# Attention and a mixture of experts in one kernel: three spaced turns of GpSimd in an attention step, and another order of the products in it

## Chip, core and metric

One core of one Trainium2 chip. The metric is the device time of an execution in microseconds, the median of several runs.

## What is computed

Sliding-window attention of 8 sequences of 576 tokens with 8 heads of 64, four heads with a plain window of 32 and four with a window that is dilated by 4, and behind it a mixture of 8 experts of which every token takes two:

```python
rel = pos[:, None] - pos[None, :]
mask_plain = (rel >= 0) & (rel < 32)
mask_dil = (rel >= 0) & (rel < 32 * 4) & (rel % 4 == 0)
scores = where(mask, q @ k.T / sqrt(64), -1e9)
attn = exp(scores - scores.max(-1)); attn /= attn.sum(-1) + 1e-9
x = (attn @ v).transpose(0, 2, 1, 3).reshape(4608, 512)

noisy = x @ w_gate + log1p(exp(x @ w_noise)) * noise
top2 = the two largest of 8;  top2_w = softmax over the two
for e in range(8):
    for k in range(2):
        rows = top2[:, k] == e
        out[rows] += top2_w[rows, k] * (relu(x[rows] @ w1[e]) @ w2[e])
```

w1 is 512 x 1024 and w2 1024 x 512 for each expert; all is fp32.

## The kernel before

**Stages.** The attention runs in 24 steps (`NS = 6 * U`). Three steps make a group of one kind of head (even groups dilated, odd plain), two groups a unit of two sequences, U = 4 units. The results x go to a scratch in DRAM (`xs`), the gate is computed in between, and each token's entry (where x lies, its weight, its row) is scattered into a table (`tab`) sorted by expert. Then the experts run one after the other (`up` and `down`): rows of x are gathered through the table, split into a high and a low part, multiplied in three fp32r products, and the results are scattered with an add into the output.

**A step.** Step i works on several tiles of 384 rows: `qk(i)` adds the mask (a product with the identity) and the scores into one PSUM tile `s` and has VectorE take the row maxima and subtract them into the SBUF tile `a` (one buffer); `expo(i)` takes the exponential on ScalarE; `ptr(i-1)` transposes the probabilities in six 128x128 blocks, ScalarE copies them out; `pv(i-1)` multiplies with v in blocks of 32 query rows, VectorE divides by the sums into `x` (three buffers); `move_x` and `store_x` bring x to its layout and to DRAM; `x_transpose(i-2)` transposes x, `gate_mm(i-2)` multiplies it with the gate's weights in blocks of 32 columns; `gate_front` transposes the logits back in three steps of every unit, when both kinds of head are there. Mask, transposes and gate_front use 128 columns of the PE array per product, scores, pv and gate_mm 32.

**Order.** The program is written in the order in which each engine executes it; there is no scheduler. The loop over i emits the parts of a step in a fixed order. Each step has two slots (2i and 2i+1, `fillers`), at which transfers and one-off work that were planned with `at(slot, ...)` are emitted; `SP` issues the loads of q, k and v, the stores of x, the clearing of the output and the weights.

**Gate.** `gate(t0, n)` is a generator for n tiles of 128 tokens. `micro(n)` advances the live generators by a few operations wherever it is called in a step (n, or 2n at `rate` 2); a `yield 1` holds one until the next slot. At its end come the scatters, one for each tile: `fill_slots(0, t)` in the generator, `fill_slots(1, t)` put into `backlog`.

**Turns of GpSimd.** A scatter or a gather of x for the first expert (`first_blocks`) needs a turn. `new_slot(scatters, speed)` is called at the end of every slot and grants turns; those left over from the slot before go to the backlog. `pool_turn` first emits a spacer: for the first turn of a grant a 1x1 copy of the latest `x` (so that GpSimd waits until it is there, `late["x"]`), otherwise a small memset (`pace`). Four turns are granted in every second slot:

```python
new_slot((4, 0)[kb % 2], 1 if kb < 28 else 2)
```

**Experts.** PE's order is `up` and `down` of blocks of rows; other work is planned with `plan(t, f)` by a clock that advances with the columns PE was given (2400 a us). For the first expert the table is read in three pieces (`idx_late`, up to rows 384, 896 and the rest), the gathers take turns, `split_first` transposes the rows on PE. What is left of the backlog is emitted by `some_of_slots` and `rest_of_slots`; from `start + 42` on the second expert's entries are read, for which all scatters must be done.

Of the kernel before, what the change touches and what calls it, by code (L numbers as in the profile page):

```python
# [25 lines left out]
U = 4  # L26
# [20 lines left out]
def attention_moe_kernel(ctx, tc, qt, kp, kd, vpl, vdl, w_gate, w_noise, noise, w1, w2, out, CAPS=(1216, 1216, 1216, 1184, 1184, 1152, 1152, 1152), SPLITS=(0, 384, 896)):  # L47
# [27 lines left out]

    late = {}
    late["stage"] = ctx.enter_context(tc.tile_pool(name="stage", bufs=2, side="right"))
# [213 lines left out]

    fresh, backlog = [True], []

    def new_slot(scatters, speed=1):
        if scatters:
            while room[0] > 0 and backlog and not experts[0]:
                pool_turn()
                backlog.pop(0)()
            room[0], fresh[0] = scatters, True
        rate[0] = speed  # L300
        held.clear()

    def pace(yes=True):

        if yes and late["x"] is not None:
            gpsimd.tensor_copy(spacer, late["x"])  # L306
        else:
            gpsimd.memset(spacer, 0.0)
# [44 lines left out]

    def qk(k):
        g, st = divmod(k, 3)
        ty = 1 - g % 2
        s = aps.tile([128, 8, 2, 64], F32, name="s", tag="s")
        for e in (0, 4):
            n = min(4, 6 - e)
            tensor.matmul(s[:, e:e + n], lhsT=identb,  # L360
                          rhs=masks[ty][:, 6 * st + e:6 * st + e + n].unsqueeze(2).to_broadcast([128, n, 2, 64]),
                          start=True, stop=False, skip_group_check=True)
        for e in range(6):
            for qd in range(4):
                if ty == 0:
                    x = qd // 2
                    b, ub = divmod(12 * st + 6 * (qd % 2) + e, 18)
                else:
                    x = qd
                    b, ub = divmod(6 * st + e, 9)  # L370
                tensor.matmul(s[32 * qd:32 * qd + 32, e], lhsT=QV[ty][:, b, x, 32 * ub:32 * ub + 32],  # L371
                              rhs=KV[ty][:, :, b, x, 32 * ub:32 * ub + 64],
                              start=False, stop=True, skip_group_check=True)
        a = sm.tile([128, 2, 6, 64], F32, name="a", bufs=1)
        mx = sm.tile([128, 6, 2], F32, name="mx")
        vector.tensor_reduce(mx, s[:, 0:6], axis=AX.X, op=OP.max)
        vector.tensor_tensor(a.rearrange("p y e c -> p e y c"), s[:, 0:6], mx.unsqueeze(3).to_broadcast([128, 6, 2, 64]), op=OP.subtract)
        SB[k] = a

    def expo(k):  # L380
# [19 lines left out]
    def pv(k):  # L400
# [3 lines left out]
        o = aps.tile([128, 2, 512], F32, name="o", tag="o")  # L404
        for hh in range(4):
            for r, a, jp, b, ub in blocks(st, ty):
                qd, c0 = (r, hh) if r < 4 else (2 * (r - 4) + hh // 2, 4 + hh % 2)
                if ty == 0:
                    y, src = hh // 2, 2 * (hh % 2) + a
                    rhs = VP[b][:, :, ub // 2, hh]  # L410
                else:
                    y, src = a, hh
                    rhs = VD[:, :, 3 * st + jp, hh, y]
                tensor.matmul(o[32 * qd:32 * qd + 32, c0 // 3, 130 * (c0 % 3):130 * (c0 % 3) + 130],
                              lhsT=pt[:, y, 128 * jp + 32 * src:128 * jp + 32 * src + 32],
                              rhs=rhs, start=True, stop=True, skip_group_check=True)
# [343 lines left out]
    X = {}  # L760
    GT = {}

    def gather(e, t):
        r0, rn = TLS[e][t] if e != "o" else (0, 128)
        g = gp_.tile([128, 4, 128], F32, name="g")
        if e == 0:

            rows = 2304 * (next((i for i in range(U - 1) if r0 + rn <= SPLITS[i]), U - 1) + 1)
            for c in range(2):
                gpsimd.indirect_dma_start(  # L770
                    out=g[0:rn, 2 * c:2 * c + 2].rearrange("p c d -> p (c d)"), out_offset=None, in_=xs[0:rows],
                    in_offset=bass.IndirectOffsetOnAxis(ap=IX[0][0][0:rn, t, c:c + 1], axis=0))
            GT[e, t] = g
            return
# [141 lines left out]
    for g in range(2 * U):  # L916
# [7 lines left out]
    fronts = {6 * u + 6 + st: (u, st) for u in range(U) for st in range(3)}  # L924
    def idx_late(before, a, b, then):
# [26 lines left out]
    def split_first(bi, t):  # L952
        xsplit(0, bi, t)()
        done[bi] += 1

# [11 lines left out]
    at(29, lambda: (new_idx(0), gens.append(idx_late(list(gens), 0, SPLITS[1], lambda: x_block(0)))))  # L967
    at(41, lambda: gens.append(idx_late(list(gens), SPLITS[1], SPLITS[2], lambda: x_block(1))))
    at(2, setup_a)
# [30 lines left out]
    def fillers(kb):  # L1000
        slot[0] = kb + 1
        for f in fill.pop(kb, []):
            f()
        new_slot((4, 0)[kb % 2], 1 if kb < 28 else 2)

    NS = 6 * U
    early[0] = False
    for i in range(NS + 2):
        slot[0] = 2 * i
        early[0] = True  # L1010
        micro(2)
# [19 lines left out]
        if 1 <= i <= NS:  # L1031
            pv(i - 1)
        micro(2)
# [8 lines left out]
    for f in fronts.values():  # L1042
        gate_front(*f)
# [34 lines left out]
    for e in range(E):  # L1078
# [19 lines left out]
        if first:  # L1098
# [22 lines left out]

            plan(start + 2.5, some_of_slots)
            plan(start + 20, lambda: gens.append(rest_of_slots()))
# [110 lines left out]
```

## Time and profile before

| | |
|---|---|
| runs | 1027.26 us median of 3 (1026.15 to 1028.05) |
| span of the profiled execution | 1086.8 us |
| attention, up to the first product of the experts | 227.24 us of the span |
| experts | 859.56 us of the span |
| busy in the span | PE 1011.7, DVE 465.7, ACT 319.4, POOL 534.5 us |
| DMA | 132.95 MB, 122 GB/s in the mean |

The profiled execution's own time is known by its span alone, from the first to the last instruction: 59.5 us more than the median of the other runs. Durations below are from it; the clock is the granted clock of TensorE, 1.00 or a half at any moment, averaged over a stretch. Busy times of an engine are without its waits. A releaser "issue" means that nothing in the profile shows what the instruction waited for, "remote" that a semaphore was awaited that no instruction of the profile is seen to raise. A `DMA_INDIRECT` of POOL is a gather or scatter, its bar the time in which the descriptors are made and not that of the transfer.

### The profile page before, as it was taken

What the parts mean: (1) busy time and instruction counts of PE and PEld (TensorE: products, weight loads), DVE (VectorE), ACT (ScalarE), POOL (GpSimd) and SP (SyncE); (2) the same over time, 40 slices, a digit from 0 to 9 for tenths busy, and PEclk for the clock granted to TensorE, in tenths of its full rate; (3) what the DMA queues carried; (4) which work ended last, traced back from release to release, by engine and by line L of the source; (5) the groups of instructions that cost most, each with busy time, mean ns of one, the idle gap of its engine ahead of it and who ended that gap; (6) DMA issues with size and microseconds to landing.
All of it is one profiled execution on the core that took longest, in us unless ns stands there. A gap on an engine that the chain in (4) does not pass through costs nothing. (4 is left out here: it accounts for less than half of the span.)

```text
span 1086.8 us, 18768 instructions
## 1 busy us (share of the span) xinstructions
PE 1011.7 (93%) x7274; PEld 855.7 (79%) x7275; DVE 465.7 (43%) x1060; ACT 319.4 (29%) x609; POOL 534.5 (49%) x727
## 2 busy tenths in 40 slices
PE   6896877778989999999999999999999999999996
PEld 4774655567878989988997889788978888888885
DVE  7673635635225444344434352435353434343221
ACT  6673534622113322222223131312131222222110
POOL 7004243455776655755644564466455645553112
PEclk9998887878999999999999999999999999999999
DMA  8898687455255243533533352426242623453123
GB/s 280 313 315 278 194 283 257 151 164 186 43 96 129 54 109 85 109 84 86 91 85 85 86 131 50 102 64 135 38 112 52 137 39 108 75 119 72 24 28 45
DMA packets 79214, 132.95 MB, mean 122 GB/s; under 512 B 31648, under 2 KB 41296, under 8 KB 77840
## 3 DMA queue, kind: packets, MB, share of 16 engines
q1 hardware_dynamic: 56768, 92.56, 27.6%
q0 software_dynamic: 22352, 39.15, 19.6%
q8 instruction: 58, 0.95, 0.4%
q14 instruction: 36, 0.29, 0.1%
HBM read 92.11 MB, written 39.54 MB: 121 GB/s over the span
## 5 line engine op out<-in xcount | busy, mean ns | idle before, releaser
L826 PE MATMUL up<-x,w1h 128*128 128x512 f32 (+4 forms) x1536 | 396.7, 344 | 10.9 <-issue 8.2
L778 POOL DMA_INDIRECT g<-xs,ixi x258 | 269.7, 1045 | 84.0 <-issue 78.6
L826 PEld LDWEIGHTS up<-x,w1h 128*128 128x128 f32 x1536 | 273.1, 189 | 37.2 <-issue 8.7
L826 PE MATMUL up<-x,w1l 128*128 128x384 f32 (+4 forms) x768 | 263.4, 343 | 0.0
L868 PE MATMUL dn<-w2h,hh 128*128 128x512 f32 x576 | 225.5, 392 | 0.0
L868 PE MATMUL dn<-w2l,hh 128*128 128x512 f32 x576 | 224.7, 390 | 0.0
L868 PE MATMUL dn<-w2h,hl 128*128 128x512 f32 x576 | 224.6, 390 | 0.0
L832 DVE SCALAR_TENSOR_TENSOR hl<-up,hh 128x384 fp32r<-128x384 f32 (+2 forms) x192 | 106.7, 557 | 249.1 <-ACT hh L830 187.0
L830 ACT ACTIVATE hh<-up 128x384 fp32r<-128x384 f32 (+4 forms) x192 | 94.6, 498 | 298.7 <-PE up L826 248.7
L845 POOL DMA_INDIRECT out_rows<-y,ixs x67 | 107.3, 1602 | 141.4 <-DVE y L877 119.0
L826 PEld LDWEIGHTS up<-x,w1l 128*128 128x128 f32 x768 | 145.4, 189 | 11.8
L877 DVE TENSOR_SCALAR y<-dn,ixs 128x512 f32<-128x512 f32 x63 | 47.3, 751 | 188.2 <-PE dn L868 163.5
L868 PEld LDWEIGHTS dn<-w2h,hl 128*128 128x128 f32 x576 | 108.4, 188 | 22.7
L868 PEld LDWEIGHTS dn<-w2h,hh 128*128 128x128 f32 x576 | 108.5, 188 | 22.0
L868 PEld LDWEIGHTS dn<-w2l,hh 128*128 128x128 f32 x576 | 108.5, 188 | 21.8
L797 ACT CAST x<-xr 128x512 fp32r<-128x512 f32 x67 | 40.5, 605 | 216.0 <-DVE xr L795 175.8
L306 POOL COPY spacer<-hh 1x1 f32<-1x1 f32 x72 | 26.4, 366 | 131.9 <-ACT hh L830 131.6
L628 POOL DMA_INDIRECT tab<-en,si x72 | 71.8, 998 | 36.1 <-issue 16.2
L798 DVE TENSOR_TENSOR x<-xr,x 128x512 fp32r<-128x512 f32 x67 | 44.7, 667 | 17.9 <-ACT x L797 12.4
L371 PE MATMUL s<-kt,qt 128*32 128x128 f32 x1152 | 41.2, 288 | 9.9 <-DMA qt<-in_qt 5.4
L371 PEld LDWEIGHTS s<-kt,qt 128*32 128x32 f32 x1152 | 32.5, 115 | 20.3 <-issue 19.6
L708 DVE TENSOR_TENSOR w1l<-ws,w1h 128x1024 fp32r<-128x1024 f32 x32 | 38.8, 1218 | 20.8 <-ACT w1h L706 10.9
(186 smaller groups left out, 867.2 us busy)
## 6 DMA issues: line engine op xcount, KB each, us to landing
ws<-in_moe_w SPq DMA_DIRECT2D x36, 512.0 KB
ws<-in_moe_w SPq DMA_DIRECT2D x112, 128.0 KB
out_rows<-zero SPq DMA_DIRECT2D x38, 256.0 KB
vd<-in_vdl SPq DMA_DIRECT2D x24, 390.0 KB
vp<-in_vpl SPq DMA_DIRECT2D x16, 585.0 KB
qt<-in_qt SPq DMA_DIRECT2D x14, 576.0 KB
xs<-x SPq DMA_DIRECT2D x24, 256.0 KB
kt<-in_kd SPq DMA_DIRECT2D x16, 320.0 KB
```

Of the source, the lines that this page charges most:

```text
L371: tensor.matmul(s[32 * qd:32 * qd + 32, e], lhsT=QV[ty][:, b, x, 32 * ub:32 * ub + 32], rhs=KV[ty][:, :, b, x, 32 * ub:32 * ub + 64], star ...
L628: ins = gpsimd.indirect_dma_start(out=tab, out_offset=bass.IndirectOffsetOnAxis(ap=si[:, kq, t:t + 1], axis=0), in_=en[:, kq, t], in_offse ...
L708: return lambda: vector.tensor_tensor(b, s, a.bitcast(F32), op=OP.subtract)
L778: gpsimd.indirect_dma_start(out=g[:, j], out_offset=None, in_=xq, in_offset=bass.IndirectOffsetOnAxis(ap=IX[e][1][:, r0 // 32 + j:r0 // 32 ...
L797: scalar.copy(xh[:, :, o:o + rn], xr[:, :, 0:rn])
L798: return lambda: vector.tensor_tensor(xl[:, :, o:o + rn], xr[:, :, 0:rn], xh[:, :, o:o + rn].bitcast(F32), op=OP.subtract)
L826: tensor.matmul(p[:, 0:n], lhsT=a[:, 128 * f:128 * f + 128], rhs=b[:, kc, 0:n], start=(i == 0), stop=(i == 11))
L830: scalar.activation(hh[:, f, 0:n], p[:, 0:n], AF.Relu)
L832: vector.scalar_tensor_tensor(hl[:, f, 0:m], p[:, 0:m], 0.0, hh[:, f, 0:m].bitcast(F32), op0=OP.max, op1=OP.subtract)
L845: ins = gpsimd.indirect_dma_start(out=out, out_offset=bass.IndirectOffsetOnAxis(ap=sc[0:rn, t, 1:2], axis=0), in_=y[0:rn], in_offset=None, ...
L868: tensor.matmul(p[0:rn], lhsT=a[:, f, o:o + rn], rhs=b[:, f % 2], start=(i == 0), stop=(i == 23))
L877: vector.tensor_scalar(y[0:rn], p[0:rn], wsc, None, op0=OP.mult)
```

## The change

It has five parts.

1. Turns: two in even slots and one in odd ones (four in each from slot 47 on). The first spacer of an odd slot copies from `a`, the difference of scores and maxima of this step, and so waits for VectorE's subtraction. A gather for the first expert is split: each half of the columns takes a turn of its own.
2. Order within a step: x_transpose (of step i-3 now, i-2 before), mask, ptr, gate_front, then scores, gate_mm (i-3), pv, with the exponential emitted behind pv. move_x is behind ptr. Fronts of the first three units come one step later.
3. pv goes over the first four blocks of rows for all four heads, and then over the last two.
4. The maxima are taken in two parts, after four and after six score blocks.
5. Gates: seven of 6 and 3 tiles in the attention (five before), double speed of `micro` from slot 16 on (28 before). Six of the slots left over are planned at 10.5 us of the experts' clock (2.5 before).

```diff
-    def new_slot(scatters, speed=1):
+    def new_slot(scatters, speed=1, at=None):
...
-            room[0], fresh[0] = scatters, True
+            room[0], fresh[0], mark[0] = scatters, True, late["x"] if at is None else at
...
-    def pace(yes=True):
+    def pace(yes=True, at=None):
+        at = late["x"] if at is None else at
-        if yes and late["x"] is not None:
-            gpsimd.tensor_copy(spacer, late["x"])
+        if yes and at is not None:
+            gpsimd.tensor_copy(spacer, at)
...
-        pace(fresh[0] and not experts[0])
+        pace(fresh[0] and not experts[0], mark[0])
...
+    def mask_scores(k):     # the two products with the identity, out of qk
...
+            if e in (3, 5):
+                e0 = e - e % 4 if e == 5 else 0
+                vector.tensor_reduce(mx[:, e0:e + 1], s[:, e0:e + 1], axis=AX.X, op=OP.max)
-        vector.tensor_reduce(mx, s[:, 0:6], axis=AX.X, op=OP.max)
...
+        late["a"] = a[0:1, 0, 0, 0:1]
...
-        for hh in range(4):
-            for r, a, jp, b, ub in blocks(st, ty):
+        bl = list(blocks(st, ty))
+        for hh, rows in [(hh, bl[0:4]) for hh in range(4)] + [(hh, bl[4:6]) for hh in (0, 2, 1, 3)]:
+            for r, a, jp, b, ub in rows:
...
-            yield from wait_turn()
-            room[0] -= 1
-            gather(0, t)
+            for c in range(2):
+                yield from wait_turn()
+                gather(0, t, c)
...
-    for t0, n, kb in ((0, 9, 17), (9, 9, 29), (18, 6, 39), (24, 3, 41), (27, 6, 51)):
+    for t0, n, kb in ((0, 6, 16), (6, 3, 18), (9, 6, 28), (15, 3, 30), (18, 6, 40), (24, 3, 42), (27, 6, 50)):
...
-        new_slot((4, 0)[kb % 2], 1 if kb < 28 else 2)
+        new_slot((2, 1)[kb % 2] if kb < NK - 1 else 4, 1 if kb < 16 else 2, late["a"] if kb % 2 else None)
...
-        if i < NS:
-            qk(i)
-        micro(2)
-        if i >= 2:
-            move_x(i - 2)
+        if 3 <= i < NS:
+            x_transpose(i - 3)
+        micro(2)
+        if i < NS:
+            mask_scores(i)
         micro(2)
         if 1 <= i <= NS:
             ptr(i - 1)
         micro(2)
+        for f in fronts.pop(i, []):
+            gate_front(*f)
+        if i >= 2:
+            move_x(i - 2)
         micro(2)
         fillers(2 * i)
         if i >= 2:
             store_x(i - 2)
-            x_transpose(i - 2)
         if i < NS:
-            expo(i)
+            qk(i)
         micro(2)
+        if 3 <= i < NS:
+            gate_mm(i - 3)
         if 1 <= i <= NS:
             pv(i - 1)
-        micro(2)
-        if i >= 2:
-            if i in fronts:
-                gate_front(*fronts.pop(i))
-            gate_mm(i - 2)
+        if i < NS:
+            expo(i)
+        for k in {NS: (NS - 3, NS - 2), NS + 1: (NS - 1,)}.get(i, ()):
+            micro(2)
+            x_transpose(k)
+            gate_mm(k)
...
-            plan(start + 2.5, some_of_slots)
+            plan(start + 10.5, some_of_slots)
...
-                    some()
-                    tick(1200)
+                    some()
+                    for t in range(*BLS[0][bi][0:2]):
+                        split_first(bi, t)
```

(`split_first` does its work only if both halves have been issued and it was not done before.)

More of the change, by code (lines that the diff above doesn't have):

```diff
@@ L74, in attention_moe_kernel @@
     ixp = ctx.enter_context(tc.tile_pool(name="ixp", bufs=3))
-    late = {}
+    late = {"x": None, "a": None}
     late["stage"] = ctx.enter_context(tc.tile_pool(name="stage", bufs=2, side="right"))
@@ L290, in attention_moe_kernel @@
     room, held, rate = [0], set(), [1]
-    fresh, backlog = [True], []
-    def new_slot(scatters, speed=1):
+    fresh, backlog, mark = [True], [], [None]
+    def new_slot(scatters, speed=1, at=None):
         if scatters:
@@ L352, in attention_moe_kernel @@
     SB, PE_, PT, XG, XT, GS = {}, {}, {}, {}, {}, {}
-    def qk(k):
+    SC = {}
+    def mask_scores(k):
         g, st = divmod(k, 3)
         ty = 1 - g % 2
-        s = aps.tile([128, 8, 2, 64], F32, name="s", tag="s")
+        s = SC[k] = aps.tile([128, 8, 2, 64], F32, name="s", tag="s")
         for e in (0, 4):
@@ L362, in qk @@
                           start=True, stop=False, skip_group_check=True)
+    def qk(k):
+        g, st = divmod(k, 3)
+        ty = 1 - g % 2
+        s = SC.pop(k)
+        mx = sm.tile([128, 6, 2], F32, name="mx")
         for e in range(6):
@@ L760, in attention_moe_kernel, with gather @@
     X = {}
-    GT = {}
-    def gather(e, t):
+    GT, GOT = {}, {}
+    def gather(e, t, c=None):
         r0, rn = TLS[e][t] if e != "o" else (0, 128)
-        g = gp_.tile([128, 4, 128], F32, name="g")
[L766 to L774, printed above, removed]
+        if e == 0:
+            GOT[t] = c == 1
+            if c == 0:
+                GT[e, t] = gp_.tile([128, 4, 128], F32, name="g")
+            rows = 2304 * (next((i for i in range(U - 1) if r0 + rn <= SPLITS[i]), U - 1) + 1)
+            gpsimd.indirect_dma_start(
+                out=GT[e, t][0:rn, 2 * c:2 * c + 2].rearrange("p c d -> p (c d)"), out_offset=None, in_=xs[0:rows],
+                in_offset=bass.IndirectOffsetOnAxis(ap=IX[0][0][0:rn, t, c:c + 1], axis=0))
+            return
+        g = gp_.tile([128, 4, 128], F32, name="g")
         if e != "o":
@@ L923, in attention_moe_kernel @@
                 at(s0 + 7 + 2 * (i // 3), f)
-    fronts = {6 * u + 6 + st: (u, st) for u in range(U) for st in range(3)}
+    fronts = {6 * u + 7 + st: [(u, st)] for u in range(U - 1) for st in range(3)}
+    fronts[6 * U + 1] = [(U - 1, 0), (U - 1, 1)]
+    fronts[6 * U + 2] = [(U - 1, 2)]
     def idx_late(before, a, b, then):
@@ L952, in split_first @@
     def split_first(bi, t):
-        xsplit(0, bi, t)()
-        done[bi] += 1
+        if GOT.get(t) and (0, t) in GT:
+            xsplit(0, bi, t)()
+            done[bi] += 1
     def x_block(bi):
@@ L962, in x_block @@
             plan(US_X[bi - 1] + 3.0 * i, lambda t=t: split_first(bi, t))
-    for t0, n, kb in ((0, 9, 17), (9, 9, 29), (18, 6, 39), (24, 3, 41), (27, 6, 51)):
+    for t0, n, kb in ((0, 6, 16), (6, 3, 18), (9, 6, 28), (15, 3, 30), (18, 6, 40), (24, 3, 42), (27, 6, 50)):
         at(kb, lambda t0=t0, n=n: gens.append(gate(t0, n)))
     L0 = 12 * (U - 1)
-    at(29, lambda: (new_idx(0), gens.append(idx_late(list(gens), 0, SPLITS[1], lambda: x_block(0)))))
-    at(41, lambda: gens.append(idx_late(list(gens), SPLITS[1], SPLITS[2], lambda: x_block(1))))
+    at(30, lambda: (new_idx(0), gens.append(idx_late(list(gens), 0, SPLITS[1], lambda: x_block(0)))))
+    at(42, lambda: gens.append(idx_late(list(gens), SPLITS[1], SPLITS[2], lambda: x_block(1))))
     at(2, setup_a)
@@ L1025, in attention_moe_kernel @@
             store_x(i - 2)
-            x_transpose(i - 2)
+        if i < NS:
[3 more added lines that the diff above has]
+            gate_mm(i - 3)
+        if 1 <= i <= NS:
+            pv(i - 1)
         if i < NS:
             expo(i)
-        micro(2)
-        if 1 <= i <= NS:
-            pv(i - 1)
-        micro(2)
-        if i >= 2:
-            if i in fronts:
-                gate_front(*fronts.pop(i))
-            gate_mm(i - 2)
+        for k in {NS: (NS - 3, NS - 2), NS + 1: (NS - 1,)}.get(i, ()):
+            micro(2)
+            x_transpose(k)
+            gate_mm(k)
         micro(2)
@@ L1041, in attention_moe_kernel @@
     early[0] = True
-    for f in fronts.values():
+    for f in sum(fronts.values(), []):
         gate_front(*f)
```

1 line of the change is left out of this document (removed).

## Prediction

> **What bounds the kernel now.** I read the page's head first, then the stage table (busy time by stretch, cut where attention steps begin), then PE's order inside one step, then the timeline of a slow step, and last the costs by line. The page: PE is the engine to follow, and its granted clock dips only in the first quarter.
>
> ```profile
> span 1086.8 us, 18768 instructions
> ...
> PE 1011.7 (93%) x7274; PEld 855.7 (79%) x7275; DVE 465.7 (43%) x1060; ACT 319.4 (29%) x609; POOL 534.5 (49%) x727
> ...
> PEclk9998887878999999999999999999999999999999
> ```
>
> Stage table: length, then busy time of PE, PEld, DVE, ACT, POOL, clock, DMA share, GB/s.
>
> ```profile
> 41.90:47.28 5.38, 5.38 (x129) 4.61 (x126) 3.40 (x8) 4.48 (x12) 0.00 (x0) 1.00 0.94 350
> 59.30:65.31 6.01, 6.01 (x137) 4.82 (x130) 3.67 (x9) 3.99 (x9) 0.00 (x0) 1.00 0.95 316
> 83.44:100.97 17.53, 11.12 (x132) 7.91 (x130) 5.21 (x17) 4.15 (x9) 8.95 (x17) 0.74 0.93 310
> 100.97:110.93 9.96, 7.70 (x134) 5.20 (x130) 2.98 (x8) 3.96 (x9) 4.12 (x7) 0.94 0.71 224
> 116.93:128.56 11.63, 7.37 (x133) 5.97 (x127) 5.24 (x20) 4.80 (x14) 4.25 (x8) 0.75 0.73 229
> 128.56:135.34 6.78, 6.16 (x139) 5.00 (x138) 5.93 (x39) 4.69 (x13) 2.22 (x4) 0.93 0.42 73
> 140.71:155.37 14.66, 9.75 (x132) 5.91 (x130) 4.18 (x13) 3.95 (x9) 8.55 (x16) 0.82 0.97 322
> 155.37:167.83 12.46, 10.06 (x133) 7.66 (x130) 4.09 (x9) 3.97 (x9) 4.26 (x8) 0.67 0.81 261
> 173.84:190.87 17.03, 9.59 (x139) 6.63 (x135) 7.38 (x46) 5.05 (x16) 8.17 (x12) 0.70 0.61 211
> 197.62:227.24 29.62, 19.76 (x250) 14.47 (x249) 14.28 (x45) 14.61 (x35) 14.42 (x25) 0.79 0.45 137
> 59.30:197.62 138.32, 108.30 (x1949) 82.23 (x1943) 73.23 (x289) 67.39 (x170) 40.69 (x73) 0.85 0.78 258
> 227.24:1086.80 859.56, 836.24 (x4153) 722.30 (x4151) 336.89 (x614) 198.33 (x336) 458.94 (x583) 0.99 0.40 88
> ```
>
> A step without work on GpSimd is all PE: 5.38 us, or 6.01 with a gate_front. The steps in which GpSimd issues four or eight scatters last 10 to 17.5 us. The experts, from 227.24 on, are PE at full clock, and the change leaves that arithmetic alone. Inside a slow step:
>
> ```profile
> 147.36 0.38 PE L414 MATMUL o<-vp,pt 128*32 128x130 f32 x2 [0.99 <-issue]
> 148.09 0.27 PE L414 MATMUL o<-vp,pt 128*32 128x130 f32 x1 [0.36 <-issue]
> ```
> ```profile
> 148.04 0.98 POOL L628 DMA_INDIRECT tab<-en,si  x1 [0.16 <-issue]
> 149.02 0.09 POOL L308 MEMSET spacer<- 1x1 f32 x1
> 149.32 0.96 POOL L628 DMA_INDIRECT tab<-en,si  x1 [0.21 <-issue]
> ```
>
> While scatters follow each other every 1.27 us, PE gets an instruction every 0.7 us and waits for nothing that the profile names. The step with two scatters (128.56) loses little.
>
> **How this stands to the runs.** The span is 59.5 us longer than the median of 1027.26, so something in this execution is not in the timed ones. The six steps above with four or more indirect transfers last 83.3 us; three clean steps of 5.38 and three or four of 6.01 in their places (12, 13, 18, 19 have a front, 15 and 21 have none) make 34.8: 48.5 us too much. The closing stretch has 29.62 us with 19.76 of PE at clock 0.79, some 14 too much, and one gap in the experts is 7.69:
>
> ```profile
> 247.75 1.01 PE L826 MATMUL up<-x,w1h 128*128 128x384 f32 x2 [7.69 <-issue]
> ```
>
> Together about 70 us of stalls of one kind, against 59.5 of excess. The experts' matmuls run back to back, so they can't give it. I conclude that nearly all of these stalls belong to the profiled execution and that some 11 us of them are left in a timed run. The forecast is for the timed run; the span itself I expect to fall more, by 30 to 50 us.
>
> **The change, part by part.**
>
> *128-column products first.* Now a step is mask (128), scores (32), transposes of p and x (128), pv (32), front (128), gate_mm (32):
>
> ```profile
> 59.30 0.50 PE L360 MATMUL s<-mask,identb 128*128 128x512 bf16 x2
> 59.73 1.52 PE L371 MATMUL s<-kt,qt 128*32 128x128 f32 x48
> 61.18 0.87 PE L396 MATMUL pp<-ident,pe 128*128 128x128 f32 x6
> 61.89 0.82 PE L449 MATMUL xtp<-ident,x 128*128 128x128 f32 x6
> 62.64 1.79 PE L414 MATMUL o<-vd,pt 128*32 128x130 f32 x48
> 64.36 0.55 PE L509 MATMUL gt<-ident,gs 128*128 128x128 f32 x3
> ```
>
> The front makes a step 0.63 longer, but three transposes are half of the six that take 0.71 (61.18 to 61.89), 0.36. The other 0.27 is two more changes between 128 and 32 columns: about 0.13 each. A step has four changes, six with a front; afterwards two. That saves 0.27 or 0.54: over steps 3 to 23 (eleven or twelve without, nine with) 8 us, if PE stays the limit.
>
> *The chain that this closes.* The transposes of p come before the next scores now, so scores, maximum, subtraction, exponential, transposes, scores is a loop within one step, where before it had a step of slack.
>
> ```profile
> L377 DVE TENSOR_TENSOR a<-s,mx 128x768 f32<-128x768 f32 x24 | 23.0, 958 | 2.4
> L376 DVE TENSOR_REDUCE mx<-s 128x12 f32<-128x768 f32 x24 | 22.9, 956 | 45.0 <-remote 20.6 <-PE s L371 12.2 <-PE xtp L449 6.2
> L382 ACT ACTIVATE pe<-a 128x768 f32<-128x768 f32 x24 | 22.6, 940 | 4.7 <-DVE a L377 4.2
> L510 DVE TENSOR_REDUCE lg<-gt 128x48 f32<-128x192 f32 x12 | 4.2, 350 | 2.7 <-PE gt L509 2.7
> ```
>
> From 192 elements (350 ns) to 768 (956) a reduction costs 1.05 ns an element and 148 ns fixed. The second part (256) is then 0.42. The loop: 0.42 + 0.96 + 0.94 + 0.71 + 1.45 (scores, 59.73 to 61.18) = 4.48, with four handovers of some 0.15 (estimate) 5.1; with a front's 0.36 between, 5.4. So the step can shrink, by 0.3 and 0.6, hardly more: the same 8 us. On ACT the copies of gate_mm stand ahead of the exponential; ACT is busy 4.0 to 4.5 of a step, so that cover is thin.
>
> *Maxima in two parts.* 24 more reductions, 148 ns each, 3.6 us of DVE; they lie under PE's last products. The Trainium skill ("Perfetto Trace Analysis", Optimizing Scalar/DVE Operations) gives about 125 ns of overhead for a VectorE instruction on PSUM and so speaks against cutting one; by it the price would be 3.0 us, and the rows agree.
>
> *Two more gates, double speed from slot 16.* A gate issues 28 small DVE operations besides those per tile, near 0.18 each:
>
> ```profile
> L540 DVE TENSOR_TENSOR l<-l,c 128x72 f32<-128x72 f32 (+2 forms) x6 | 1.2, 204 | 0.3
> L557 DVE TENSOR_TENSOR wd<-u 128x9 f32<-128x9 f32 (+2 forms) x6 | 0.9, 158 | 0.0
> ```
>
> That is 5 us a gate, 10 in all. From 59.30 to 197.62 DVE is busy 73.2 us in 15 steps, 4.9 a step. With 10 and 2.2 more it is 5.7, over PE's new 5.1 to 5.4. Here DVE takes over, and of the 5.8 us that the order saves in these steps I keep half; the early steps keep 2. Order, chain and gates together: -5.
>
> *Turns.* Four a step at once become two and one, the one behind the subtraction. Bounds: 0, if timed runs have none of these stalls, to -11, what is left of them. I take -5, near the middle, since two scatters cost little in 128.56. The e=0 gathers take a turn for each half, 14 for 7 tiles. Some 12.5 steps of three turns and five half-steps of four are 57; less 14 gathers, 43 scatters before the experts. Now, up to 230 us:
>
> ```profile
> tab<-en,si POOLq DMA_INDIRECT x44
> g<-xs,ixf POOLq DMA_INDIRECT x8
> ```
>
> So nothing is pushed into the experts, and six gathers less (7.6 us) stand ahead of the gap at 247.75. The six later slots planned at 10.5 for 2.5 are GpSimd's alone.
>
> *The new wait.* `a` has one buffer, and GpSimd reads it: the next subtraction waits for that copy, and behind it in DVE's queue pv's divisions, then all of PE. GpSimd is held in places:
>
> ```profile
> POOL g L770 <- DMA ixf<-tab: 6.2, 1, 6.2
> POOL g L770 <- DMA out_rows<-zero: 5.1, 1, 5.1
> ```
>
> The copy has a step (5.4) less two turns (2.5), so a hold of 6.2 costs 3.3 and shorter ones nothing: 0 to 7 us; I take 1.
>
> *Moves.* x_transpose and gate_mm one step later put one more pair into the tail (0.75 + 0.47): 0 to +1.2, +1 taken. move_x goes behind pt's copies (0.86), so SP's stores start that much later, with loads behind them; SP has slots of 5 us, so 0. More issues of spacers are covered by GpSimd's idle time. pv in groups of four: 24 products in six groups either way, 0.
>
> Sum: -5 - 5 + 1 + 1 = -8: 1019.
>
> **Rivals.**
> 1. *The stalls are real.* Then spacing gains most of the 48.5: at 0.7 of it, -34, with the rest about 985. For it: the same sort of gap appears in the experts. Against: the 59.5 us has no other home. The Trainium skill ("Runtime: NRT & Kernel Launch", The ~15µs preamble/postamble breakdown) states that a profile's total exceeds the reported time by some 6 us whatever the kernel; by that rule the stalls would be real. Here the excess is ten times that.
> 2. *DVE eats all.* If gates bind every step from 8 on and timed runs have no stalls, the gains are 2 against 2: 1027. For it: 5.7 against 5.4. Against: DVE's gate work is partly ahead of the loop, not in it.
> 3. *Slower: the wait on `a`.* It decides once GpSimd holds the subtraction for over 10 us in sum: three holds of 3.3, or 0.6 in each of 17 steps. Five such holds give 1019 + 15 = 1034. For it: one buffer, and scatters that wait for a gate's slot numbers stand in the same queue. Against: from 116.93 to 135.34 GpSimd is busy 6.5 of 18.4 us, so it catches up.
>
> **How the numbers follow.** Forecast (1006 to 1024) 0.50; stalls real 0.12; DVE eats all 0.15; slower 0.23. 0.2% (2 us) is about what a measurement tells from no change: faster 0.62, same 0.15, slower 0.23. The range leaves out most of the first rival and the far end of the third: 1004 to 1032.
>
> **What would show it.** Right: clean steps of 5.0 to 5.2 us, and 5.3 to 5.6 with a front; score products directly followed by gate_mm and pv; no stretch of PE at 0.7 us an instruction; transposes of p waiting for the exponential by under 0.3; DVE busiest in steps 8 to 23. Wrong: the subtraction waiting for GpSimd's copy; steps of 6 and more with GpSimd idle; a gap in the experts before the second block; or a timed gain as large as the span's.

## The result and the profile after

| | time | against the kernel before |
|---|---|---|
| before | 1026.70 us | |
| after | 1056.52 us median (1053.43 to 1059.05) | 1.0277 [1.0243, 1.0311], slower |

The forecast was 1019, the range ended at 1032. The change is 30 us slower. The profiled execution of the changed kernel took 1057.19 us, its span is 1.7 us less.

The page of the changed kernel (span, busy time by engine, granted clock in 40 slices):

```profile
span 1055.5 us, 18851 instructions
...
PE 986.0 (93%) x7276; PEld 843.5 (80%) x7277; DVE 476.7 (45%) x1140; ACT 321.7 (30%) x615; POOL 535.1 (51%) x737
...
PEclk8999997889999999999999999999999999999999
```

Its stage table (start and end, length, then busy time of PE, PEld, DVE, ACT, POOL, clock, DMA share, GB/s): a step without a front, one with, a step with a front and a gate's work, step 21, and the experts.

```profile
41.16:47.10 5.94, 5.13 (x129) 4.28 (x127) 3.57 (x9) 4.40 (x12) 0.00 (x0) 1.00 0.85 259
59.51:65.77 6.26, 5.45 (x132) 4.66 (x130) 3.91 (x10) 3.82 (x9) 0.42 (x1) 1.00 0.88 306
72.01:83.89 11.88, 7.48 (x138) 6.42 (x136) 8.60 (x49) 5.59 (x17) 0.00 (x0) 0.86 0.79 274
161.06:178.75 17.69, 7.81 (x139) 6.45 (x136) 9.40 (x54) 6.49 (x18) 6.76 (x13) 0.77 1.02 377
210.69:1055.50 844.81, 831.51 (x4154) 719.78 (x4152) 337.26 (x610) 199.01 (x336) 457.42 (x590) 0.99 0.41 90
```

PE's busy time in the first two (5.13 and 5.45) is what the forecast had for the whole step, but both steps are 0.81 us longer than that. Waits of PE, then of DVE, up to the end of attention (each row: who waits, `<-` whom it waits for, then total, times, longest):

```profile
PE s L380 <- DVE mx L385: 34.6, 24, 4.3
PE xtp L461 <- ACT xt L463: 10.1, 5, 6.8
```
```profile
DVE a L387 <- POOL spacer L307: 6.8, 1, 6.8
```

And PE's score products in the step at 41.16, then the second part of them in step 9 (72.01):

```profile
42.26 1.08 PE L380 MATMUL s<-kt,qt 128*32 128x128 f32 x32
44.15 0.65 PE L380 MATMUL s<-kt,qt 128*32 128x128 f32 x16 [0.81 <-DVE mx L385]
...
78.27 1.08 PE L380 MATMUL s<-kt,qt 128*32 128x128 f32 x16 [3.78 <-DVE mx L385]
```

The 48 score products are cut in 32 and 16: after the fourth block TensorE stands until VectorE has taken the first maximum. This happens in each of the 24 steps, by 0.81 us where VectorE is free, by 3.8 us in step 9, where gate operations stand ahead of that maximum, and by 4.3 at most. The DVE row is one hold in step 21, of VectorE's subtraction by GpSimd's copy out of `a`; the longest wait of the `xtp` row (6.8 us) lies behind it.

### The profile page after: what moved, and what is told of

Read it like the earlier page. It is cut to its first block, busy times and chain, and to the rows that moved or that the text cites. A ratio compares the mean times of both kernels' runs of the same rounds, so it can differ in the third digit from the quotient of the medians.

```text
span 1055.5 us, 18851 instructions
## 1 busy us (share of the span) xinstructions
PE 986.0 (93%) x7276; PEld 843.5 (80%) x7277; DVE 476.7 (45%) x1140; ACT 321.7 (30%) x615; POOL 535.1 (51%) x737
## 5 line engine op out<-in xcount | busy, mean ns | idle before, releaser
L380 PE MATMUL s<-kt,qt 128*32 128x128 f32 x1152 | 45.6, 294 | 36.1 <-DVE mx L385 34.6
```

## The experiments

Ratios are against the kernel before, run between the others on the same chip. e15, e16 and e17 ran once each and have no ratio; like e9 and e10, which ran twice, they are read by their steps.

| run | what | ratio [95%] |
|---|---|---|
| e1 | before, repeated | 0.9996 [0.9968, 1.0024] |
| e2 | before + maximum cut in two | 1.0246 [1.0229, 1.0263] |
| e3 | after, one maximum | 1.0095 [1.0076, 1.0114] |
| e4 | after, scores in two tiles | 1.0110 [1.0093, 1.0127] |
| e5 | e3, turns read from x | 1.0039 [1.0021, 1.0058] |
| e6 | e4, turns read from x | 1.0036 [1.0017, 1.0055] |
| e7 | e5, five gates | 1.0093 [1.0060, 1.0126] |
| e8 | e7, old turns | 1.0060 [1.0035, 1.0085] |
| e9 | before, first gate 12 slots later | 1.0235 [1.0187, 1.0282] |
| e10 | e8, first gate 12 slots later | 1.0306 [1.0259, 1.0352] |
| e11 | before, front ahead of ptr | 1.0040 [1.0017, 1.0063] |
| e12 | e5, single speed | 1.0037 [1.0018, 1.0057] |
| e13 | before, fewer loads | 0.9919 [0.9893, 0.9945] |
| e14 | e5, fewer loads | 0.9979 [0.9957, 1.0000] |
| e18 | e6, five gates spread thin | 1.0104 [1.0071, 1.0136] |

### Were the stalls of the first profile real? (e1)

> The kernel before, unchanged, for a second profile. Theory A (the stalls next to runs of scatters are an accident of the first profiled execution): the span comes near the timed runs, 1025 us, attention ends near 180 us, and steps with scatters last 5.4 to 7 us. Theory B (profiling always stalls this kernel): a span of 1080 to 1090 and steps of 10 to 17 us again. The time itself is 1027 by both.

The page of e1, and its stage table (a step without a front; a step with a front, and with five scatters by GpSimd; the experts):

```profile
span 1022.0 us, 18768 instructions
...
PE 983.3 (96%) x7274; PEld 836.7 (82%) x7275; DVE 466.7 (46%) x1060; ACT 319.8 (31%) x609; POOL 533.3 (52%) x727
```
```profile
39.88:45.26 5.38, 5.38 (x130) 4.60 (x127) 3.40 (x8) 4.45 (x12) 0.00 (x0) 1.00 0.93 293
87.42:93.42 6.00, 6.00 (x135) 4.81 (x130) 4.03 (x10) 4.08 (x9) 5.00 (x9) 1.00 1.01 256
179.85:1022.00 842.15, 829.88 (x4154) 717.38 (x4151) 337.84 (x614) 198.70 (x336) 457.39 (x583) 1.00 0.41 90
```

No: a step in which GpSimd issues five scatters is 6.00 us of pure PE. The span of this execution, 1022.0, is what the changed kernel's 1055.5 has to be held against: 30.8 of the 33.5 us lie in attention (210.69 against 179.85), 2.7 in the experts.

### The maximum in two parts (e2, e3, e4)

e2 is the kernel before with this part alone, e3 the changed kernel without it:

```diff
             if e in (3, 5):                          # e2 adds, e3 takes away
                 e0 = e - e % 4 if e == 5 else 0
                 vector.tensor_reduce(mx[:, e0:e + 1], s[:, e0:e + 1], axis=AX.X, op=OP.max)
-        vector.tensor_reduce(mx, s[:, 0:6], axis=AX.X, op=OP.max)   # e3 has this
```

> The kernel before with the maxima in two parts and nothing else. Theory 1 (the cut maximum makes PE wait: the products of score blocks 4 and 5 go into the PSUM tile that VectorE reads for the first maximum): 0.8 us in each of 24 steps, more in those with a gate, so 1046 to 1055 us. Theory 2 (the loss is in the new order and the gates; the cut maximum alone is 3.6 us of VectorE in hidden places): 1026 to 1029.

> The changed kernel with one maximum over all six blocks. Theory 1 in its simple form: the 34.6 us of PE's waits for the maximum go, and nothing comes instead: 1022. Theory 2 (the closed loop is the bound): the maximum of 0.96 stands whole in the loop, and PE waits about 0.7 us a step for the exponential at the transposes of p instead: 1045 to 1058.

PE's longest wait in e2:

```profile
PE s L372 <- DVE mx L377: 33.6, 24, 4.8
```

The cut alone makes the kernel before 25 us slower (2.46%), as its first theory said; taking it out of the changed kernel gives 18.7 us back (2.77% to 0.95%). e3's 1037 us lie between its two theories: the waits for the maximum are gone, but something else is left. e4 keeps two maxima but gives them a PSUM tile of one bank each:

```diff
-        s = SC[k] = aps.tile([128, 8, 2, 64], F32, name="s", tag="s")
+        s = SC[k] = [aps.tile([128, 4, 2, 64], F32, name=f"s{i}", tag=f"s{i}") for i in range(2)]
...
-                vector.tensor_reduce(mx[:, e0:e + 1], s[:, e0:e + 1], axis=AX.X, op=OP.max)
+                vector.tensor_reduce(mx[:, e0:e + 1], p[:, 0:n], axis=AX.X, op=OP.max)
+                vector.tensor_tensor(a[:, :, e0:e + 1]..., p[:, 0:n], mx..., op=OP.subtract)
```

> The changed kernel with the scores in two PSUM tiles of one bank each (blocks 0 to 3, 4 and 5), each with its own maximum and subtraction: nothing that PE writes is being read. Theory 1: PE's waits for the maximum are gone, clean steps last 5.1 us and 5.45 with a front, gate steps keep about half of their excess: 1025 to 1038. Theory 2: two more VectorE instructions a step make it no faster than 1056.

A step of e4 without a front, PE's score products and VectorE's first maximum in it:

```profile
43.77 1.52 PE L381 MATMUL s<-kt,qt 128*32 128x128 f32 x48
44.91 0.69 DVE L386 TENSOR_REDUCE mx<-s 128x8 f32<-128x512 f32 x1 [1.49 <-PE s L381]
```

The 48 products run through to 45.29 while VectorE takes the first maximum from 44.91 on. No wait of PE for a maximum is left in e4, and this step (42.36 to 47.59) is 5.23 us, although VectorE has one more operation in it than in the changed kernel. The time is 1039 us, 1 us above the first theory's range. In both kernels the maximum of blocks 0 to 3 and the products of blocks 4 and 5 touch different banks; what differs is that in the changed kernel they lie in one tile. So what bound them was the wait that goes with the tile: a product that writes a tile waits for the instruction ahead of it in the program that reads it. The Trainium skill ("PSUM — Partial Sum Buffer", PSUM bank collisions raise a hardware error) says to guard PSUM by bank and quadrant; by that rule no guard was needed here, and e4 agrees.

### The copy out of `a` (e3 to e6)

e3 and e4 were still 1% slower than before. DVE's wait in e3, GpSimd's order there, and step 21:

```profile
DVE a L386 <- POOL spacer L307: 9.0, 1, 9.0
```
```profile
138.38 0.17 POOL L307 COPY spacer<-a 1x1 f32<-1x1 f32 x1
153.56 1.01 POOL L782 DMA_INDIRECT g<-xs,ixf  x1 [15.01 <-issue]
...
157.15 0.18 POOL L307 COPY spacer<-a 1x1 f32<-1x1 f32 x1
```
```profile
142.26:161.41 19.15, 6.14 (x139) 5.09 (x137) 9.51 (x54) 7.00 (x18) 6.75 (x12) 0.74 1.02 365
```

GpSimd stands for 15 us at the first gather, which needs the positions `ixf` read from the table (the profile names no releaser here, so that this read is what it waits for is argued from its place); the copy out of `a` comes three transfers later, at 157.15, and the subtraction of step 21 behind it. TensorE is then idle for 12.7 us, and the clock falls to 0.50 during the gap and is still there at the end of the step (mean 0.74). e5 and e6 take all turns' copies from x:

```diff
-        new_slot(..., 1 if kb < 16 else 2, late["a"] if kb % 2 else None)
+        new_slot(..., 1 if kb < 16 else 2)
```

> The changed kernel with one maximum (as in e3), and with every spaced turn of GpSimd read from x, none from `a`: new_slot's third argument of odd slots is left out. Theory A (what e3 still lost is one hold: GpSimd waits 15 us at the first gather for the positions, the copy out of `a` is queued behind it, the subtraction of step 21 waits for the copy): step 21 falls from 19.2 us to about 7, its 12.7 us gap ahead of the transposes of x goes, half clock in it goes; 1037 - 12 = about 1025 us (1021 to 1028). Rival B (step 21 waits for the gate's work or for the positions anyway): the gap moves to another operand, x or xt, and the time stays above 1033.

> The scores in two PSUM tiles with a maximum and a subtraction each (as in e4), and no turn read from `a`. Theory A: 1039 - 13 = about 1026 us, step 21 at 7 to 8 us; against e5 the two maxima and two subtractions cost some 0.4 us of VectorE a step, and the exponential may begin earlier: 0 to +3 us against e5. Rival B: above 1034, as in e5. If an early maximum is worth anything once TensorE does not wait for it, this is below e5 by 2 us or more.

```profile
143.27:153.18 9.91, 5.84 (x139) 4.83 (x137) 9.43 (x54) 6.96 (x18) 0.00 (x0) 1.00 1.03 372
```

In e5 GpSimd does nothing in the whole of step 21 (0.00; it still stands 15 us at the first gather), and nobody waits for it: the step takes 9.91 us. But the time falls by 5.8 us (0.95% to 0.39%), not by the 12 expected, and lands between theory A and rival B: of 9.2 us won in step 21, 4.2 are lost in step 23 (21.2 us in e3 up to the first product of the experts, 25.4 in e5), which does the gate's last work. e6 stands as e5 does: two tiles with an early first maximum are worth nothing more.

### The other parts undone (e7, e8, e12)

```diff
-    for t0, n, kb in ((0, 6, 16), (6, 3, 18), (9, 6, 28), (15, 3, 30), (18, 6, 40), ...   # e7, e8
+    for t0, n, kb in ((0, 9, 18), (9, 9, 30), (18, 6, 40), ...
-        new_slot((2, 1)[kb % 2] if kb < NK - 1 else 4, 1 if kb < 16 else 2)
+        new_slot((2, 1)[kb % 2] if kb < NK - 1 else 4, 1 if kb < 28 else 2)               # e7; e12: 44
+        new_slot((4, 0)[kb % 2], 1 if kb < 28 else 2)                                     # e8
```

> e5 with the gate as before in number and speed: five pieces (9, 9, 6, 3, 6 groups), begun when the fronts have come, and double speed from slot 28 on. Rival C (the two more gates and the double speed cost: gate steps of 8 to 9 us in e3 against 6.8 to 7.8 before): 3 to 6 us below e5. Theory A (the gates' work is the same per group and only its place differs): within 2 us of e5; two gates fewer save about 2 x 30 small VectorE operations.

> e7 with the turns as before too, four of them in each even slot and none in the odd: what is left of the change is the order of the products and transposes, the gathers of one column each, and the later start of the up products' slots. If spaced turns are worth the 5 us that I put on them, this is 5 us above e7; if bursts of indirect transfers cost only a few us in an undisturbed execution (before, repeated: 0.5 to 1.5 us in steps with five of them), 0 to 3 us above. Against the kernel before this run is the order alone: 8 + 5 us of gain by the prediction's terms, so 1013 to 1016; by the steps of e3 and of the repeated run of before (5.7 against 6.0 to 6.5 us) about 24 x 0.4 = 9 us less what the closing steps give back, 1018 to 1026.

> e5 (one maximum, turns read from x) with single speed up to slot 44 in place of 16, seven gates as before in this kernel. Theory C (double speed puts some 30 gate operations ahead of one maximum, and the closed loop pays for each): the gate steps 9, 15 and 21 of 8.9, 9.0 and 9.9 us fall to 6 to 7 with 1 us more in their neighbours, 3 to 6 us below e5, about 1027 us and no better than before. If the same work costs the same wherever it stands: within 2 us of e5. If the gates' results now come too late for the first block of an expert: slower than e5, with the gap ahead of the first up products.

All three expectations of a gain failed. Five gates are 5.5 us slower than seven, not faster. The speed is worth nothing: 1.0037 against 1.0039. The turns are worth nothing that can be told (e8 against e7: 1.0060 and 1.0093, intervals overlap). And e8, called the order alone here (pv's order, the split gathers and the later slots are still in it), is 0.6% slower than before, where I had expected 1013 to 1016 us by the prediction's terms and 1018 to 1026 by the steps of e3. Its trace says where: steps 4 to 20 take 104.2 us against 106.5 in e1, a gain of 2.2, but steps 21 to 23, up to the first product of the experts, take 46.7 against 39.1, and the experts 846.9 against 842.2. In e7 these are 44.8 and 849.0, in e5 41.8 and 843.8: with the gate in seven pieces e5 is the faster there, presumably because less of the gate's work is left for the end. So the order had to be looked at by itself, in steps without a gate.

### The order without the gate's work (e9, e10, e11)

e9 and e10 begin the first gate 12 slots later, so that steps 9 to 14 have none of its work; only these steps are read.

```diff
-    for t0, n, kb in ((0, 9, 17), (9, 9, 29), ...        # e10: from 18 to 30 in e8
+    for t0, n, kb in ((0, 9, 29), (9, 9, 29), ...
```

> The kernel before with the first gate (groups 0 to 8) begun at slot 29 in place of 17, so that attention steps 9 to 14 have no gate's work on VectorE. Read from this run are those six steps, beside the same six of e10; the time itself may rise, since the gate's work comes later in a lump. In the repeated run of before the six steps took 36.1 us with the gate. Without it: three of 5.4 and three of 6.0 with a front, 34.2 us.

> The order alone (e8: old turns, five gates, one maximum) with the first gate begun at slot 30, so that steps 9 to 14 have no gate's work; in e8 they took 36.0 us with it. Theory D (the order does gain some 0.5 us a step, and the gate's VectorE work eats it, since maximum and subtraction now stand in a loop that closes within the step): three of 4.9 and three of 5.3 to 5.7, 30.6 to 31.8 us, 2.4 to 3.6 below e9. Rival E (the order gains nothing over six steps, gate or not): within 0.5 of e9.

Stage tables of e9 and e10, steps 9 to 14:

```profile
65.25:101.58 36.33, 34.94 (x772) 28.34 (x766) 21.52 (x48) 25.33 (x62) 0.00 (x0) 1.00 0.98 341
```
```profile
66.86:102.57 35.71, 32.81 (x767) 27.92 (x765) 21.95 (x49) 26.16 (x63) 0.00 (x0) 1.00 0.97 337
```

PE's busy time falls by 2.13 us in six steps, 0.36 a step, near the forecast's 2.4. The time falls by 0.62, a little more than rival E's 0.5. PE idles 2.90 us in the new order and 1.39 in the old, most of it in gaps that the profile does not name, as in e10:

```profile
87.02 0.40 PE L482 MATMUL pp<-xt,wg 128*32 128x128 f32 x6
88.21 0.41 PE L482 MATMUL pp<-xt,wg 128*32 128x128 f32 x8 [0.80 <-issue]
```

The packet records show what these gaps have in common: packets of 16,384 bytes in an instruction queue begin at 74.25, 79.66, 85.86 and 91.95, and e10's four unnamed gaps end at 76.53, 82.11, 88.21 and 94.33, each 2.3 to 2.5 us later. e9's two gaps end 2.2 and 2.3 us after such a packet. Not every packet has a gap: each of the two stretches has six, of which two in e10 and five in e9 pass without one (e9's first gap follows a packet at 64.96). By the Trainium skill ("Perfetto Trace Analysis", The 4-stage abstract model) an instruction has 64 bytes, so a packet would hold 256, an estimate. A step has about 128 products and as many weight loads, and the six steps have six such packets, which agrees.

e11 moved the front alone, in the kernel before:

```diff
+        if i in fronts:
+            gate_front(*fronts.pop(i))
         if 1 <= i <= NS:
             ptr(i - 1)
```

> The kernel before with one move: the front's three transposes stand ahead of the transposes of p instead of behind pv, so a step with a front has two changes of product shape less, and no chain gets shorter. By the prediction's 0.13 us a change: 12 fronts x 0.27 = 3.2 us, ratio 0.997. If the 0.27 was not the change of shape but waiting at that place, nothing: 1.000 within 0.002. If VectorE's reduction of the front, now ahead of more of the step's work, delays that: slower by up to 2 us.

PE's wait in e11, up to the end of attention:

```profile
PE xtp L449 <- ACT xt L451: 9.8, 10, 1.8
```

Steps with a front became 6.8 us where they had been 6.0, and the run is 4 us slower, outside all three expectations: the second transposes of x now wait for ScalarE, since the front takes one of the PSUM buffers that they use. A new wait took the place of the two changes of shape, so their price was not measured by this run.

### Fewer loads (e13 to e16)

Two groups' v is loaded and the loads for the other six are left out, so the later steps work on old values of v.

```diff
-        if g + 1 < 2 * U:
+        if g + 1 < 2:
             for i, f in enumerate(v_loads(g + 1)):
```

> The kernel before without the loads of v for all but the first two groups of blocks (left out: six of eight; the attention works on with the first ones' values, so the work and its order stay). Theory F (the DMA engines' load makes TensorE's instructions late): the unnamed gaps of before (0.6 us at 71.6, 1.0 at 121.7 and 135.4) go, DMA share in steps 4 to 20 from 0.97 to about 0.6; steps go to 5.4 and 6.0 where no gate is; 3 to 6 us below before. Rival G (fetches have nothing to do with it): the gaps stay and the time is within 2 us of before.

> e5 without the same loads of v. Theory F: e5's gaps at gate_mm and at the scores (1.15, 1.04, 0.70 us) go, and the order's gain comes out: it falls by more than the kernel before does, by 6 to 10 us, and ends 0 to 5 us below e13. Rival G: as far above e13 as e5 is above before, some 4 us.

> e10 (the order alone, no gate work in steps 9 to 14) without the same loads of v. Read are steps 9 to 14, 35.7 us in e10 with four unnamed gaps. Theory F: the gaps go, three steps of 4.9 and three of 5.3 to 5.7, 30.6 to 31.8 us. Rival G: 35 or more.

> e9 (the order of before, no gate work in steps 9 to 14) without the same loads of v; steps 9 to 14 were 36.3 us in e9 with two unnamed gaps. Theory F: 34.2 us, three of 5.4 and three of 6.0, so that the two orders differ by 2.4 to 3.6 us here where they differed by 0.6. Rival G: 36 or more.

Stage tables of e16 (old order: steps 9 to 14, and one without a front), then of e15 (new order, the same):

```profile
65.44:99.61 34.17, 34.17 (x773) 28.27 (x766) 21.56 (x48) 25.31 (x62) 0.00 (x0) 1.00 0.74 243
70.83:76.21 5.38, 5.38 (x129) 4.61 (x127) 3.40 (x8) 4.44 (x11) 0.00 (x0) 1.00 0.73 207
```
```profile
64.87:98.31 33.44, 31.68 (x767) 27.14 (x765) 21.36 (x48) 25.25 (x63) 0.00 (x0) 1.00 0.72 232
70.59:75.98 5.39, 5.11 (x128) 4.34 (x126) 3.27 (x8) 4.34 (x12) 0.00 (x0) 1.00 0.64 187
```

With the DMA share at 0.74 the old order has no gap at all: PE is busy for 34.17 of 34.17 us, the 34.2 expected. So the unnamed gaps come with the full DMA. The kernel before is 8 us faster without these loads (0.9919), more than the 3 to 6 expected, of which the profiles show 4.7 in steps 4 to 20 (101.7 us in e13, 106.5 in e1). In the new order the gaps go too, all but one of 0.33, and yet a step stays at 5.39 us, not 4.9; the six steps, 33.44, lie between the two expectations. PE in that step of e15, then VectorE and ScalarE in it:

```profile
71.36 0.87 PE L406 MATMUL pp<-ident,pe 128*128 128x128 f32 x6 [0.28 <-ACT pe L392]
72.17 1.52 PE L380 MATMUL s<-kt,qt 128*32 128x128 f32 x48
...
76.78 0.33 PE L406 MATMUL pp<-ident,pe 128*128 128x128 f32 x1 [0.31 <-ACT pe L392]
```
```profile
73.78 0.96 DVE L384 TENSOR_REDUCE mx<-s 128x12 f32<-128x768 f32 x1 [1.94 <-PE s L380]
74.84 0.96 DVE L386 TENSOR_TENSOR a<-s,mx 128x768 f32<-128x768 f32 x1
75.83 0.90 ACT L392 ACTIVATE pe<-a 128x768 f32<-128x768 f32 x1 [0.70 <-DVE a L386]
```

From 71.36 to 76.78 runs the closed loop: transposes of p, scores, maximum, subtraction, exponential, and the transposes again, which wait for it by 0.28 and 0.31 (in five of these six steps). Its 5.4 us are as long as the old step. With a front, which stands inside the loop, it is 5.73 against 6.01.

e14 is again slower than e13 (0.9979 and 0.9919, some 6 us, against the 0 to 5 faster of theory F), so these gaps are not what separates e5 from the kernel before. Stage tables of e13, then e14: steps 4 to 20, 9 to 11, 15 to 17:

```profile
37.27:139.01 101.74, 98.93 (x2194) 80.95 (x2190) 74.06 (x249) 72.85 (x182) 33.36 (x63) 1.00 0.73 225
66.06:83.65 17.59, 16.48 (x394) 14.07 (x389) 15.40 (x74) 13.87 (x38) 0.00 (x0) 1.00 0.60 192
101.66:120.56 18.90, 17.24 (x395) 14.07 (x389) 15.85 (x74) 13.92 (x38) 6.46 (x12) 1.00 0.64 198
```
```profile
37.02:143.39 106.37, 94.69 (x2191) 80.37 (x2189) 78.79 (x299) 74.45 (x188) 33.24 (x61) 0.97 0.67 209
64.78:87.25 22.47, 17.74 (x394) 14.98 (x392) 19.77 (x100) 15.51 (x42) 5.13 (x10) 0.92 0.56 181
103.83:126.58 22.75, 18.14 (x394) 15.01 (x392) 19.50 (x97) 15.28 (x42) 9.86 (x18) 0.92 0.54 169
```

The six steps with gate work take 8.7 us more in the new order (45.22 against 36.49), the other eleven 4.1 less. Part of both is that the fronts come a step later: of the nine that lie in these eleven steps of e13, e14 has six there, two are in gate steps (9 and 15) and one is behind. By the clean steps a front is 0.63 us in the old order and 0.34 in the new, so some 1.9 of the 4.1 and 0.7 of the 8.7 us are the fronts' move (an estimate). Without it the order with its seven gates wins 0.2 us in a step without gate work and loses 1.3 in a step with it. Some of the loss is the two gates more (VectorE is busy 4.7 us longer in steps 4 to 20); the order alone, e8, takes 3.7 us more in the same six steps (41.0 against 37.2 in e1), without the fronts' move 0.5 each. The old order pays for the gate as well: its 37.2 us stand against 32.3 for six clean steps of 5.38. The reason is in the queues, here PE's and VectorE's in step 9 of e5:

```profile
68.03 1.52 PE L380 MATMUL s<-kt,qt 128*32 128x128 f32 x48
```

```profile
71.63 0.26 DVE L283 TENSOR_SCALAR free<-free 128x98 int32<-128x98 int32 x1
71.75 0.95 DVE L384 TENSOR_REDUCE mx<-s 128x12 f32<-128x768 f32 x1
72.74 0.96 DVE L386 TENSOR_TENSOR a<-s,mx 128x768 f32<-128x768 f32 x1
```

The scores end at 69.55, and the maximum starts at 71.75, since gate operations run without a break ahead of it. In the old order the transposes of p that follow in a step belong to the step before, so such a delay has some slack; in the loop it is paid at once. That this is the whole of the difference was not tried.

### A shorter loop, and thin gates (e17, e18)

e17 is e15 with e4's two tiles; e18 is e6 with five gates and `micro` at half speed up to slot 40.

```diff
-        new_slot(..., 1 if kb < 16 else 2)
+        new_slot(..., 0 if kb < 40 else 1 if kb < 44 else 2)     # e18
```

> e15 (the order alone, fewer loads of v, no gate work in steps 9 to 14) with the scores in two PSUM tiles as in e4, so that only the second tile's maximum and subtraction (4 of 12 columns of groups, 0.42 and 0.43 us by the reductions' rate, for 0.96 and 0.96) stand between scores and exponential. Theory H (the closed loop sets the steady step): the loop falls by up to 1 us until TensorE's 4.9 and 5.2 set it; steps 9 to 14, 33.4 us in e15, come to 30.6 to 31.6, and the 0.3 us waits of the transposes for the exponential go. Rival J (something else in the order makes the 5.4): 33 or more, with the waits where they were.

> e6 (two tiles, turns read from x) with five gates, and the gate's work at half speed up to slot 40, single to 44, double after: some 9 small operations a step, 1.6 to 2 us of VectorE, in place of 16 to 32. Theory H: the gate steps of 9 to 10 us go, steps 9 to 20 become 5 to 6 us each, 6 to 10 us less in these steps than e6's 86; the tables come later, so some of it is given back ahead of the experts: 1020 to 1030 us in all, and if no more than 5 us are given back it beats the kernel before. If the late tables delay the first block by more: 1030 to 1040, with the loss between step 20 and the first up products.

One step of e17, with a front, and VectorE in it:

```profile
92.31:97.86 5.55, 5.45 (x131) 4.67 (x129) 3.89 (x11) 3.98 (x10) 0.00 (x0) 1.00 0.87 294
```
```profile
95.18 0.69 DVE L386 TENSOR_REDUCE mx<-s 128x8 f32<-128x512 f32 x1 [0.68 <-PE s L381]
...
97.03 0.42 DVE L387 TENSOR_TENSOR a<-s,mx 128x256 f32<-128x256 f32 x1
```

Steps 9 to 14 take 32.94 us where e15 took 33.44: between the two expectations. The working of mine was wrong: the first tile's two operations end at 96.66, after the last score product, so VectorE is done only some 0.2 us earlier than with one maximum (97.45 against scores that end near 95.55, 1.9 us; in e15 75.80 against 73.69, 2.1). The step is shorter by just that: 5.55 for 5.73, and the waits of the transposes for the exponential are gone. So the loop does set the steady step of e15, as far as one execution of each can show it.

When these two ran, the kernel before took 1083 us on a chip on which e1 had found it at 1026; so of their times the ratio and the steps are used. e18 is 1.0% slower than before, which for 1027 us would be 1038, in its second expectation (an estimate); but the loss is not only behind step 20: steps 9 to 20 take 91.4 us where e6's, on another chip, took 78.0. TensorE again pauses while GpSimd's scatters are under way, as in the first profile of the kernel before, spaced turns or not; PE and GpSimd in its step 15:

```profile
109.92 0.38 PE L484 MATMUL pp<-xt,wg 128*32 128x128 f32 x2 [0.99 <-issue]
```
```profile
107.95 0.97 POOL L641 DMA_INDIRECT tab<-en,si  x1 [0.16 <-issue]
109.23 0.96 POOL L641 DMA_INDIRECT tab<-en,si  x1 [0.22 <-issue]
```

The scatters again follow each other every 1.3 us: a spacer whose value is already there when GpSimd comes to it holds nothing up. The same distance between scatters did no harm in e1, so it is not enough by itself to bring such pauses about. None of the versions beats the kernel before.

## Why the prediction was wrong

- *Maxima in two parts*: **the step that failed.** It priced 3.6 us of VectorE under PE's products and did not ask what the products behind the first maximum wait for. VectorE's time was priced well (4.2 us more in e2 than in e1); the wait of TensorE, 34.6 us in all, was put at nothing. It costs 18.7 us of the 30 (e3), 25 alone (e2).
- *The new wait*: right in its place, `a` with one buffer and a gather that is held, and too small. 0 to 7 us were given and 1 taken, from a hold of 6.2; the hold is 15 us, and VectorE waits 6.8 (after) and 9.0 (e3). It is worth 5.8 us of time (e3 to e5).
- *128-column products first*: its size was right, 0.36 us a step of PE's time (2.13 over steps 9 to 14, predicted 2.4), its condition "if PE stays the limit" was not met.
- *The chain that this closes*: the step that hid this. I let the step shrink by 0.3 and 0.6 to a loop of 5.1 and 5.4, which needs a cut maximum that costs PE nothing. With one maximum the loop is 5.39 and 5.73 (e15), against the old 5.38 and 6.01: nothing without a front, 0.3 with one. The 0.15 us of a handover had no row behind it; in e15 an operation of the loop starts 0.03 to 0.10 us behind the end of the one before.
- *Two more gates, double speed*: "DVE takes over" was right as a mechanism. The two gates' time on VectorE was put too high, 10 us for a measured 6.2 (472.9 us busy in e5, 466.7 in e7, 56 operations more), and its effect too low: it is not VectorE's sum over a step that counts but what stands ahead of the maximum, some 0.5 us a gate step in the order alone (e8), 1.3 with the seven gates (e14). The second rival, that VectorE eats all, describes the order best, and did not go far enough. Yet the two gates more are a gain over all, not a cost (e7 against e5), most likely since less is left for the end, and the speed is neither (e12).
- *Moves*: 0 to +1.2 was given for one more pair of transposes and gate products in the tail. From step 21 to the experts the new order takes 2.7 us more in e5 and 7.6 in e8; which of the moved parts does it was not tried.
- *Turns*: -5 was taken between 0 and -11; the runs cannot tell it from the bound 0 (e8 against e7).
- *How this stands to the runs* was right: the stalls of the first profile are not in a run of 1027 us (e1). Its 34.8 us for the six steps are two of 5.38 and four of 6.01, not three and three or four as it says. The stalls were not one execution's accident, though: e18 met such pauses again. By the Trainium skill ("Runtime: NRT & Kernel Launch", The ~15µs preamble/postamble breakdown) a profile's total lies some 6 us above the reported time. The record gives no such total, only the span from the first to the last instruction, and that lies 1.7 us below the reported time in both e1 (1022.0 and 1023.65) and the changed kernel, so the runs neither bear the rule out nor speak against it.
- The clean steps came out as forecast in PE's busy time, and two signs of being wrong are what the profile shows: the subtraction waiting for GpSimd's copy, and steps of 6 us and more with GpSimd idle. The third rival, at 1034, was the slowest and the range ended short of it, at 1032, since no rival had TensorE wait for a maximum.

The sum: 18.7 for the maximum, 5.8 for the copy, 4.0 left in e5 (0.39%), together the 2.77% of 1027; each is the difference between neighbours in the row before, e5, e3, after, so they add up by construction, and each is known to some 2 to 4 us. The single spans of e5 and e1 differ by 6.9 us: 3.1 before step 4, 2.7 behind step 20, 1.7 in the experts, and -0.5 in steps 4 to 20. The first of these varies by 3 us among runs of the old order (step 4 begins at 34.3 in e1 and 37.3 in e13), so the split of the 4.0 stays open.

## What to carry to other kernels

When an operation is cut so that its first part can start early, look at what the producer must do afterwards in the same tile: the early reader becomes a wait for the writer, unless the parts have tiles of their own. When a reordering closes a loop within one step, add up the whole loop against the old step, and count every small operation that an engine of the loop has queued ahead of it. A spacer that reads a value with one buffer makes the engine that writes it wait for everything queued ahead in the reader.

## What the runs showed of the hardware

TensorE stood for 0.2 to 1.2 us without a wait that the profile names where the DMA engines were 97 and 98% busy (e10, e9), each time until 2.2 to 2.5 us after a packet of 16,384 bytes in an instruction queue had begun; at a share of 0.74 the old order lost nothing (e16), though six such packets fall into its six steps too. That these packets are TensorE's instructions, and that it stands for want of them, is inferred from the times. In the session of e17 and e18 all 16 runs of the kernel before took 1076 to 1089 us, in place of 1024 to 1032 on the same chip in the session of e1, and TensorE paused by about 1 us while GpSimd issued scatters (e18); what brings this on stays open.
